# Attention and ReGLU in one kernel: the values of batches 0, 1 and 2 by casting transfers from GpSimd's queue

## The chip, the cores and the metric

The kernel runs on one core of a Trainium2 chip. A core has five engines with instruction queues of their own: TensorE (PE in the profile) for matrix products and for transposes by an identity matrix, VectorE (DVE), ScalarE (ACT), GpSimd (POOL) and SyncE (SP), which here only issues DMA transfers. Each engine takes its instructions in the order of the program, so an instruction that waits holds everything behind it on its engine. The transfers of all queues run on the same 16 DMA engines of the core. The metric is the device time of one execution in microseconds; smaller is better.

## The reference

Eight batches of eight heads, 576 positions, head size 64, all float32. Attention is causal by blocks of 64 positions; its output, turned into 4608 rows of 512, goes through a gated feed-forward layer (FFN).

```
scores = (q @ k^T) / sqrt(64)          # 8 x 8 x 576 x 576
scores = where(block_i >= block_j, scores, -1e9)
attn   = exp(scores - max) / sum
x      = (attn @ v) as 4608 x 512
out    = (relu(x @ w_gate) * (x @ w_val)) @ w_out     # 512 -> 1536 -> 512
```

q, k and v are 9.4 MB each, the three weights 3.1 MB each, and the output 9.4 MB. Matrix products are made in bfloat16, so each input has to be turned from float32 to bfloat16 somewhere between DRAM and TensorE.

## The kernel before, in words

**Tiles.** The 576 positions of a batch are 512 main ones (four chunks of 128) and a tail of 64. A round `r` is one pair of heads of one batch (batch `r // 4`, pair `r % 4`). For a round TensorE makes the scores, transposed, keys on the partitions (`part` for the rounds of batch 0, `visit` after that), ScalarE the exponentials into `attnT`, VectorE or GpSimd sets the masked corners to zero (`corners`), and TensorE multiplies `attnT` with the values (`products_with_v`, L585 main, L599 tail). A 65th column of ones in each head's values gives the sum of the exponentials, by which VectorE divides (`normalise`). The result is transposed into `xT` and is the moving operand of the FFN products: L663 for gate and value, L748 for the output. ScalarE takes the ReLU (L673), VectorE the product `hT` (L679) and the copy of the output (L758).

**Values.** `v_bf` has two buffers, for even and odd batches, 128 partitions x 5 chunks x 8 heads x 65 columns of bfloat16; chunk 4 is the tail. The tail products of batches 0 to 2 are made apart (`tail_visit`, `tail_av` with L547), some time behind the main ones.

**How q, k and v come in.** For batches 3 to 7, `load_qkv` issues casting transfers from GpSimd's queue: the source is float32, the destination bfloat16, one transfer per chunk of 128 positions and 8 heads (L338). For batches 0, 1 and 2 the class `Early` loads float32 into staging buffers from SyncE's queue and casts them on an engine:

- `load_qk` (L140) and `cast_qk` (L195) for q and k. Batches 0 and 1 are then transposed on TensorE (`pe_mains`), batch 2 by SyncE's DMA transposes into `perm` (`transpose`, L242) and copies of these into `qTm` and `kTm` (`unpermute`, L253);
- `load_v` (L159), one transfer per head, and `cast_v` (L220) for the values of batches 0 and 1: per pair of heads in batch 0, per four heads in batch 1;
- `load_v_chunks` (L169) and `cast_v_chunks` (L228), per two chunks, for the values of batch 2;
- `load_tails` and `cast_tails` for the 64 tail positions of all three.

The pool `stage` has ten buffers of 4 KB per partition. Loads of q, k, v and of the weights (L356, cast by L382) and the exponentials of the separate tails (L499) take their turns in it. A transfer into a buffer waits until that buffer's last cast is over. Each queue's completion semaphores are eight in turn, so the ninth transfer of a queue waits for the landing of the first.

**Order.** Nothing is scheduled by the compiler here. The table `AT` gives each action a place, counted in FFN matmuls (negative ones lie before the first), and the actions are issued in the order of these numbers, with FFN matmuls between them as far as the number says. It's an order of issue and not a time: each engine's queue gets its own instructions in this order and runs ahead as far as its waits let it. Names in it that matter here: `Lq..` and `Lv..` load q, k and v of batch 0, `E1..` and `E2..` those of batches 1 and 2, `cq..` and `cv..` cast those of batch 0, `ev..` the values of batch 1, `q2` and `q24` cast and DMA-transpose the first and second half of q and k of batch 2, `u0` to `u3` copy `perm` into `qTm` and `kTm` (`u0` on GpSimd, `u1` and `u2` on VectorE, `u3` on VectorE and ScalarE), `A0` and `B0` are the tail products of batch 0, `v2` casts the values of batch 2, `s8` to `s11` are the scores of batch 2, `l3` and `lv3` load batch 3.

```
for n in sorted(acts, key=lambda n: AT[n]):
    ffn(int(AT[n]) - place[0])
    place[0] = max(place[0], int(AT[n]))
    acts[n]()
```

Of the kernel before, what the change touches and what calls it, by code (L numbers as in the profile page):

```python
# [17 lines left out]
def kernel(  # L18
# [10 lines left out]
    nc = tc.nc  # L29
# [40 lines left out]
    v_bf = [consts.tile([128, NCH, 8, 65], BF, name=f"v_bf{i}") for i in range(2)]  # L70
# [4 lines left out]
    def halves_of(t, par):  # L75

        return t[64 * par : 64 * par + 64].rearrange("p (h g) d -> p g h d", g=2)[
            :, par
        ]
# [29 lines left out]
    def new_bt():  # L109
        return sb.tile([64, 512], BF, name="q_bt", bufs=2)  # L110

    def new_stage(w):
        return sb.tile([128, 1024], FP, name="stage", bufs=10)[:, 0:w]
# [7 lines left out]
    class Early:  # L121
# [32 lines left out]
            self.load(self.st[1, h0], k, h0, n, k_eng)  # L154

        def load_v(self, h0, n):
            st = self.st[2, h0] = new_stage(256 * n)
            for h in range(n):
                nc.sync.dma_start(  # L159
                    st[:, 256 * h : 256 * h + 256].rearrange("p (c d) -> p c d", c=4),  # L160
                    v[self.b, h0 + h, 0:512, :].rearrange("(c p) d -> p c d", p=128),
                )

        def load_v_chunks(self, g):

            st = self.st["c", g] = new_stage(1024)
            for i in range(2):
                s0 = 256 * g + 128 * i
                nc.sync.dma_start(  # L169
                    st[:, 512 * i : 512 * i + 512].rearrange("p (h d) -> p h d", h=8),  # L170
                    v[self.b, :, s0 : s0 + 128, :].rearrange("h p d -> p h d"),
                )

        def load_tails(self, ts):
# [27 lines left out]
        def cast_tails(self, q_too, par, eng):  # L202

            if q_too:
                self.tl = new_bt()
                eng(self.tl, self.st["t", 0])
            eng(
                k_bt[self.b % 2][
                    64 * par : 64 * par + 64, :, 64 * par : 64 * par + 64
                ],  # L210
                self.heads_of(1, par),
            )
            par = 1 - par
            eng(
                halves_of(v_bf[self.b % 2][:, 4, :, :], par)[:, :, 0:64],
                self.heads_of(2, par),
            )

        def cast_v(self, h0, n, eng):
            eng(  # L220
                v_bf[self.b % 2][:, 0:4, h0 : h0 + n, 0:64].rearrange(
                    "p c h d -> p h c d"
                ),
                self.st[2, h0].rearrange("p (h c d) -> p h c d", h=n, c=4),
            )

        def cast_v_chunks(self, g, eng):
            eng(  # L228
                v_bf[self.b % 2][:, 2 * g : 2 * g + 2, :, 0:64],
                self.st["c", g].rearrange("p (c h d) -> p c h d", c=2, h=8),  # L230
            )

        def half(self, t, hg):
# [566 lines left out]
    dve, act, pool = nc.vector.tensor_copy, nc.scalar.copy, nc.gpsimd.tensor_copy  # L800
# [7 lines left out]
    with tc.manual_schedule(engines={E.PE, E.DVE, E.Activation, E.Pool, E.SP}):  # L808

        e0, e1, e2 = [Early(b) for b in range(3)]  # L810
# [45 lines left out]
        zeros_by = {"dve": zero_dve, "pool": zero_pool}  # L856

        def v_2():
            e2.cast_v_chunks(0, pool)
            e2.cast_v_chunks(1, pool)  # L860

        def un(hp):
            return lambda: e2.unpermute(hp, [by[e] for e in HOW[f"u{hp}"]])
# [27 lines left out]
        def mains_1(hp):  # L891
# [8 lines left out]
        AT = {  # L900
            "Lq0": -63.5,
            "Lq2": -62.27,
            "Lv0": -61.59,
            "Lv2": -59.5,
            "Lq6": -59.5,
            "Lq4": -59.5,
            "v00": -58.48,
            "g00": -56.5,
            "Lv4": -54.8,
            "Lv6": -54.8,  # L910
            "g01": -53.5,
            "v10": -53.5,
            "g10": -49.5,
# [14 lines left out]
            "c0": -37.69,  # L928
            "M1k": -37.69,
            "M1q": -37.69,  # L930
            "cv2": -33.09,
            "p11": -32.5,
            "p10": -29.72,
            "M2": -29.71,
            "p12": -29.71,
            "cv0": -29.7,
            "p20": -20.67,
            "p21": -20.67,
            "M3": -20.67,
# [5 lines left out]
            "p22": -20.26,  # L945
            "a1": -17.73,
            "p30": -17.27,
            "cv4": -17.27,
            "b1": -17.03,
            "p32": -13.98,  # L950
            "c2": -13.74,
# [5 lines left out]
            "cg00/23": -4.5,  # L957
            "b2": -4.5,
            "cg01/23": -3.47,
            "cv6": -3.23,  # L960
            "v20": -0.39,
            "g11": -0.39,
            "cv00/01": 4.09,
# [20 lines left out]
            "w11": 32.11,  # L984
            "w20": 32.12,
            "w10": 32.12,
            "E1v0": 32.16,
            "w21": 32.16,
            "E1q6": 32.19,
            "E1q4": 32.19,  # L990
            "E1v4": 32.19,
            "T0": 32.19,
            "E2q0": 32.19,
            "T1": 32.23,
# [6 lines left out]
            "cw21/0": 32.33,  # L1001
            "cw11": 32.33,
            "cw20": 32.33,
            "ev0": 32.33,
            "q6": 32.36,
            "q4": 32.36,
            "E2q4": 33.82,
            "ev4": 34.05,
            "tc0": 34.05,
            "q2": 37.71,  # L1010
            "tc1": 48.64,
# [2 lines left out]
            "m0": 83.51,  # L1014
            "m1": 87.1,
            "s4": 93.79,
            "E2v0": 109.09,
            "cw21/1": 110.84,
            "e4": 114.3,
            "c4": 116.83,  # L1020
# [3 lines left out]
            "e5": 121.28,  # L1024
            "m2": 122.6,
            "c5": 124.67,
            "E2v4": 125.35,
            "T2": 126.26,
            "a5": 127.05,
            "s6": 128.09,  # L1030
# [25 lines left out]
            "L1": 184.04,  # L1056
            "u1": 190.06,
            "u0": 190.06,
            "v2": 191.07,
            "q24": 191.07,  # L1060
            "E1": 194.6,
            "s8": 198.81,
# [121 lines left out]
        acts = {  # L1184
            "Lq0": lambda: e0.load_qk(0, 2, nc.scalar),
            **{f"Lq{h}": lambda h=h: e0.load_qk(h, 2) for h in (2, 4, 6)},
            **{f"Lv{h}": lambda h=h: e0.load_v(h, 2) for h in (0, 2, 4, 6)},
            **{
                n: load(n, load_w_half, i, g, t)
                for i in range(2)  # L1190
# [20 lines left out]
            "j2": lambda: junk(1, 256),  # L1211
            "cq0": lambda: e0.cast_qk(0, 2, (dve, act)),
            **{f"cq{h}": lambda h=h: e0.cast_qk(h, 2, (pool, pool)) for h in (2, 4, 6)},
            **{f"cv{h}": lambda h=h: e0.cast_v(h, 2, pool) for h in (0, 2, 4, 6)},
            "M0": lambda: e0.pe_mains(0, (dve, [(act, 0, 1), (dve, 1, 4)])),
            "M1q": lambda: e0.pe_mains(1, [by[e] for e in HOW["M1"]], ts=(0,)),
            "M1k": lambda: e0.pe_mains(1, [by[e] for e in HOW["M1"]], ts=(1,)),
# [22 lines left out]
            "T2": lambda: load_tails(e2),  # L1240
            "E2q0": lambda: e2.load_qk(0, 4),
            "E2q4": lambda: e2.load_qk(4, 4),
            "E2v0": lambda: e2.load_v_chunks(0),
            "E2v4": lambda: e2.load_v_chunks(1),
            "q0": lambda: e1.cast_qk(0, 4, (pool, None)),
            "k0": lambda: e1.cast_qk(0, 4, (None, by[HOW["k0"]])),
            "q4": lambda: e1.cast_qk(4, 2, [by[e] for e in HOW["q4"]]),
            "q6": lambda: e1.cast_qk(6, 2, [by[e] for e in HOW["q6"]]),
            "ev0": lambda: e1.cast_v(0, 4, pool),
            "ev4": lambda: e1.cast_v(4, 4, pool),  # L1250
            **{f"tc{b}": lambda e=e: e.cast_tails(True, 0, pool) for b, e in enumerate((e0, e1, e2))},
            **{f"td{b}": lambda e=e: e.cast_tails(False, 1, dve) for b, e in enumerate((e0, e1, e2))},
            **{f"m{hp}": lambda hp=hp: mains_1(hp) for hp in range(4)},
# [4 lines left out]
            **{f"o{i}": lambda: late.pop(0)() for i in range(4)},  # L1258
            **{f"u{hp}": un(hp) for hp in range(4)},
            "v2": v_2,  # L1260
            "l3": lambda: load_qkv(3, (0, 1)),
            "t2": e2.transpose_tails,
# [61 lines left out]
```

## Time and profile before

| what | us |
|---|---|
| median of three runs | 362.74 (362.61 to 365.04) |
| span of the profiled execution, first to last instruction | 363.3 |
| TensorE busy | 353.3 |
| TensorE's weight loads busy (beside its products) | 176.9 |
| VectorE busy | 170.7 |
| ScalarE busy | 167.9 |
| GpSimd busy | 112.8 |

The times come from runs without a profile; every duration of one instruction, and every place in time, comes from the one profiled execution. Its span is 0.6 us above the median. In the profile a line of a group or of a timeline names engine, source line, operation, the tile written and the tiles read, the shape and the number of instructions; `[2.42 <-DMA x]` says that the engine sat idle 2.42 us before it and that the transfer of x ended that. A transfer counts as landed when its semaphore says so, later than its issue by the time given under DMA issues: the median is 5.4 us for the float32 loads of v from SyncE's queue, and 6.1 us for the casting loads of v from GpSimd's. The DMA engines' work by queue over the whole span:

```profile
q0 software_dynamic: 70480, 8.85, 46.7%
q1 hardware_dynamic: 76480, 31.86, 44.8%
q10 hardware_dynamic: 5088, 8.78, 7.2%
```

The columns are packets, MB written, and the time that the packets took, as a share of 16 engines' span. q0 is GpSimd's queue, q1 SyncE's and q10 ScalarE's.

### The profile page before, as it was taken

What the parts mean: (1) busy time and instruction counts of PE and PEld (TensorE: products, weight loads), DVE (VectorE), ACT (ScalarE), POOL (GpSimd) and SP (SyncE); (2) the same over time, 40 slices, a digit from 0 to 9 for tenths busy, and PEclk for the clock granted to TensorE, in tenths of its full rate; (3) what the DMA queues carried; (4) which work ended last, traced back from release to release, by engine and by line L of the source; (5) the groups of instructions that cost most, each with busy time, mean ns of one, the idle gap of its engine ahead of it and who ended that gap; (6) DMA issues with size and microseconds to landing.
All of it is one profiled execution on the core that took longest, in us unless ns stands there. A gap on an engine that the chain in (4) does not pass through costs nothing.

```text
span 363.3 us, 7423 instructions
## 1 busy us (share of the span) xinstructions
PE 353.3 (97%) x2933; PEld 176.9 (49%) x2933; DVE 170.7 (47%) x426; ACT 167.9 (46%) x265; POOL 112.8 (31%) x157
## 2 busy tenths in 40 slices
PE   7899999999998999999999999999999999999996
PEld 3544455545544555555555454554455544444443
DVE  4663456677433363444445443554255434333432
ACT  4933676696325850666055625553365403302310
POOL 4647645695209500680049001930000000000000
PEclk9999999999999999999999999999999999999999
DMA  8999999999999995899449951997220130031013
GB/s 245 298 357 374 314 239 255 189 156 138 186 203 108 141 154 137 56 146 186 109 49 145 169 133 46 130 157 152 81 16 14 54 102 0 0 88 29 1 41 105
DMA packets 152083, 49.97 MB, mean 138 GB/s; under 512 B 134512, under 2 KB 145008, under 8 KB 152048
## 3 DMA queue, kind: packets, MB, share of 16 engines
q0 software_dynamic: 70480, 8.85, 46.7%
q1 hardware_dynamic: 76480, 31.86, 44.8%
q10 hardware_dynamic: 5088, 8.78, 7.2%
q8 instruction: 23, 0.38, 0.5%
q14 instruction: 12, 0.10, 0.1%
HBM read 37.75 MB, written 9.44 MB: 130 GB/s over the span
## 4 chain that ended last, share of the span: by engine, by line
PE 89%; DMA 5%; ACT 4%; DVE 1%; issue 0%; POOL 0%; SPq 0%; POOLq 0%; DVEq 0%
PE ffnp L663 49%; PE ffnp L748 23%; PE sc L450 3%; PE ffnp L585 2%; PE one L450 2%; DMA xT<-xnat 2%; DMA stage<-in_moe_w_gate_dram 2%; PE one L585 2%; ACT attnT L414 2%; PE one L663 1%; ACT attnT L455 1%; PE ffnp L547 1%; PE one L794 1%; DMA kTt<-k_bt 1%; PE ffnp L599 1%; PE one L599 1%
## 5 line engine op out<-in xcount | busy, mean ns | idle before, releaser
L679 DVE TENSOR_TENSOR hT<-gate_sb,ffnp 128x512 bf16<-128x512 bf16 x106 | 72.6, 685 | 96.5 <-PE ffnp L663 70.7
L673 ACT ACTIVATE gate_sb<-ffnp 128x512 bf16<-128x512 f32 x103 | 62.1, 605 | 103.3 <-PE ffnp L663 93.6
L663 PE MATMUL ffnp<-xT,wv 128*128 128x512 bf16 x376 | 100.7, 379 | 0.0
L663 PE MATMUL ffnp<-xT,wg 128*128 128x512 bf16 x364 | 99.0, 379 | 1.1 <-DMA xT<-xnat 0.4
L748 PE MATMUL ffnp<-wo,hT 128*128 128x512 bf16 (+2 forms) x444 | 98.8, 373 | 0.0
L748 PEld LDWEIGHTS <-hT 128*128 128x128 bf16 x444 | 41.8, 98 | 45.5 <-issue 0.6
L663 PEld LDWEIGHTS <-wv 128*128 128x128 bf16 x432 | 40.1, 98 | 45.5 <-issue 3.2
L663 PEld LDWEIGHTS <-wg 128*128 128x128 bf16 x432 | 39.8, 98 | 44.6 <-issue 3.6
L455 ACT ACTIVATE attnT<-sc 128x1024 bf16<-128x1024 f32 x56 | 56.8, 1044 | 0.0
L758 DVE COPY ob<-ffnp 128x512 f32<-128x512 f32 (+2 forms) x37 | 25.0, 676 | 45.1 <-PE ffnp L748 44.7
L338 POOL DMA_DIRECT2D q_bf<-in_q_dram x20 | 17.8, 903 | 76.3 <-DVE hT L679 52.0
L462 ACT ACTIVATE attnT<-one 128x512 bf16<-128x512 f32 (+1 forms) x28 | 15.0, 536 | 53.8 <-PE ffnp L450 53.8
L585 PEld LDWEIGHTS <-attnT 128*128 128x128 bf16 x640 | 26.5, 97 | 13.9 <-DVE attnT L803 1.3
L338 POOL DMA_DIRECT2D v_bf<-in_v_dram x30 | 24.3, 853 | 6.8 <-PE one L585 2.2
L450 PEld LDWEIGHTS <-kTm 64*128 64x128 bf16 x384 | 11.3, 94 | 15.6 <-issue 7.8
L338 POOL DMA_DIRECT2D k_bf<-in_k_dram x20 | 17.7, 933 | 0.0
L450 PE MATMUL sc<-qTm,kTm 64*128 64x512 bf16 (+1 forms) x168 | 16.9, 305 | 0.0
L585 PE MATMUL ffnp<-v_bf,attnT 128*128 128x65 bf16 x320 | 15.0, 194 | 0.0
L462 ACT ACTIVATE attnT<-ffnp 128x512 bf16<-128x512 f32 (+1 forms) x28 | 15.0, 534 | 0.0
L803 DVE MEMSET attnT<- 64x128 uint32 x59 | 9.0, 165 | 12.0 <-ACT attnT L455 10.2
L524 DVE TENSOR_TENSOR xnat<-ffnp,recip 128x256 bf16<-128x256 f32 x32 | 13.6, 424 | 1.1
L585 PE MATMUL one<-v_bf,attnT 128*128 128x65 bf16 x250 | 11.6, 193 | 0.7 <-POOL v_bf L220 0.7
(122 smaller groups left out, 293.8 us busy)
## 6 DMA issues: line engine op xcount, KB each, us to landing
out_dram<-ob ACTq DMA_DIRECT2D x29, 256.0 KB, 2.4
stage<-in_moe_w_val_dram SPq DMA_DIRECT2D x6, 512.0 KB, 8.2
stage<-in_moe_w_gate_dram SPq DMA_DIRECT2D x6, 512.0 KB, 8.7
stage<-in_moe_w_out_dram SPq DMA_DIRECT2D x6, 512.0 KB, 10.5
q_bf<-in_q_dram POOLq DMA_DIRECT2D x20, 128.0 KB, 4.3
k_bf<-in_k_dram POOLq DMA_DIRECT2D x20, 128.0 KB, 5.8
v_bf<-in_v_dram POOLq DMA_DIRECT2D x20, 128.0 KB, 6.1
stage<-in_v_dram SPq DMA_DIRECT2D x19, 128.0 KB, 5.4
```

Of the source, the lines that this page charges most:

```text
L338: ins = nc.gpsimd.dma_start(dst, part_of)
L450: nc.tensor.matmul(o, kTm[b % 2][head_of(hh), c, hp, :], qT, start=True, stop=True)
L455: return lambda: nc.scalar.activation(at[:, :, lo : lo + 512], sc, AF.Exp, scale=scale)
L462: nc.scalar.activation(at[:, hh, 1024 : 1024 + w], third[hh][:, 0:w], AF.Exp, scale=scale)
L524: nc.vector.tensor_tensor(out=out, in0=av[:, 0:m, 0:64], in1=recip[:, 0:m].to_broadcast([rows, m, 64]), op=AX.mult,)
L585: nc.tensor.matmul(av[:, p, :], at[:, col : col + 128], v_bf[b % 2][:, c, h, :], start=(p == 0), stop=(c == p), skip_group_check=True,)
L663: nc.tensor.matmul(to, (wg, wv)[t][f // 4][:, c, 128 * (f % 4) : 128 * (f % 4) + 128], x[:, c], start=(c == 0), stop=(c == 3),)
L673: nc.scalar.activation(gate_sb, gate, AF.Relu)
L679: nc.vector.tensor_tensor(out=h, in0=gate_sb, in1=val, op=AX.mult)
L748: nc.tensor.matmul(op, hT[f][:, 128 * s : 128 * (s + 1)], wo[f // 4][:, f % 4, n0:n1], start=(f == 0), stop=(f == 11),)
L758: nc.vector.tensor_copy(ob, op)
L803: nc.vector.memset(o, 0.0)
```

## The change

The main values (chunks 0 to 3) of batches 0, 1 and 2 come by casting transfers from GpSimd's queue, straight into `v_bf`, one per chunk and group of heads: four transfers for all heads of batch 0, four for each half of the heads of batch 1, four for batch 2. The loads from SyncE's queue, their staging buffers and the eight casts on GpSimd are gone. Places in the table change with it: batch 0's values are one action, placed directly before the casts of q and k; batch 1's two actions stand among the casts of the output weights; batch 2's `v2` now issues the transfers, and stands at 184.5 in place of 191.07, so before `u0` and `q24`, where its casts stood behind them.

```diff
         def load_v(self, h0, n):
-            st = self.st[2, h0] = new_stage(256 * n)
-            for h in range(n):
-                nc.sync.dma_start(
-                    st[:, 256 * h : 256 * h + 256].rearrange("p (c d) -> p c d", c=4),
-                    v[self.b, h0 + h, 0:512, :].rearrange("(c p) d -> p c d", p=128),
-                )
-
-        def load_v_chunks(self, g):
...
+            for c in range(4):
+                nc.gpsimd.dma_start(
+                    v_bf[self.b % 2][:, c, h0 : h0 + n, 0:64],
+                    v[self.b, h0 : h0 + n, 128 * c : 128 * c + 128, :].rearrange(
+                        "h p d -> p h d"
+                    ),
                 )
...
-        def cast_v(self, h0, n, eng):
...
-        def cast_v_chunks(self, g, eng):
...
         def v_2():
-            e2.cast_v_chunks(0, pool)
-            e2.cast_v_chunks(1, pool)
+            e2.load_v(0, 8)
...
-            "Lv0": -61.59,
-            "Lv2": -59.5,
+            "Lv0": -47.0,
...
-            "Lv4": -54.8,
-            "Lv6": -54.8,
...
-            "cv2": -33.09,
...
-            "cv0": -29.7,
...
-            "cv4": -17.27,
...
-            "cv6": -3.23,
...
-            "E1v0": 32.16,
+            "E1v0": 32.325,
...
-            "E1v4": 32.19,
+            "E1v4": 32.335,
...
-            "ev0": 32.33,
...
-            "ev4": 34.05,
...
-            "E2v0": 109.09,
...
-            "E2v4": 125.35,
...
-            "v2": 191.07,
+            "v2": 184.5,
...
-            **{f"Lv{h}": lambda h=h: e0.load_v(h, 2) for h in (0, 2, 4, 6)},
+            "Lv0": lambda: e0.load_v(0, 8),
```

More of the change, by code (lines that the diff above doesn't have):

```diff
@@ L156, in load_v @@
         def load_v(self, h0, n):
-            st = self.st[2, h0] = new_stage(256 * n)
-            for h in range(n):
-                nc.sync.dma_start(
-                    st[:, 256 * h : 256 * h + 256].rearrange("p (c d) -> p c d", c=4),
-                    v[self.b, h0 + h, 0:512, :].rearrange("(c p) d -> p c d", p=128),
-                )
-        def load_v_chunks(self, g):
[L166 to L171, printed above, removed]
+            for c in range(4):
[4 more added lines that the diff above has]
+                    ),
                 )
@@ L216, in cast_tails @@
                 self.heads_of(2, par),
-            )
-        def cast_v(self, h0, n, eng):
[L220 to L225, printed above, removed]
-        def cast_v_chunks(self, g, eng):
-            eng(
-                v_bf[self.b % 2][:, 2 * g : 2 * g + 2, :, 0:64],
-                self.st["c", g].rearrange("p (c h d) -> p c h d", c=2, h=8),
             )
@@ L1213 @@
             **{f"cq{h}": lambda h=h: e0.cast_qk(h, 2, (pool, pool)) for h in (2, 4, 6)},
-            **{f"cv{h}": lambda h=h: e0.cast_v(h, 2, pool) for h in (0, 2, 4, 6)},
             "M0": lambda: e0.pe_mains(0, (dve, [(act, 0, 1), (dve, 1, 4)])),
@@ L1242 @@
             "E2q4": lambda: e2.load_qk(4, 4),
-            "E2v0": lambda: e2.load_v_chunks(0),
-            "E2v4": lambda: e2.load_v_chunks(1),
             "q0": lambda: e1.cast_qk(0, 4, (pool, None)),
@@ L1248 @@
             "q6": lambda: e1.cast_qk(6, 2, [by[e] for e in HOW["q6"]]),
-            "ev0": lambda: e1.cast_v(0, 4, pool),
-            "ev4": lambda: e1.cast_v(4, 4, pool),
             **{f"tc{b}": lambda e=e: e.cast_tails(True, 0, pool) for b, e in enumerate((e0, e1, e2))},
```

## The prediction

> **What bounds the kernel now.** First the page's busy times, then its idle groups by stretch: TensorE is the bound, with 353.3 of 363.3 us, at full granted clock in all slices.
>
> ```profile
> PE 353.3 (97%) x2933; PEld 176.9 (49%) x2933; DVE 170.7 (47%) x426; ACT 167.9 (46%) x265; POOL 112.8 (31%) x157
> ```
>
> By stretch TensorE is busy 13.45 of the first 17.43 us (much of it one-off waits between small products), 5.01 of 5.57 up to 23 us, all 37.00 up to 60, 42.63 of 43 up to 103, 15.45 of 17 up to 120 and all 180 after that up to 300. So the order of TensorE's work is fixed and full; any delay put into it before 120 us moves the end one for one, and only a wait that is taken out before 120 us can be won. Two places matter.
>
> **Start.** The chain that ended last, in order of time, goes through a weight transfer here:
>
> ```profile
> 12.98 6.80 DMA stage<-in_moe_w_gate_dram
> 19.80 0.62 ACT wg L382
> 20.42 0.49 ACT xT L629
> 20.96 0.38 PE ffnp L663
> ```
>
> ScalarE ends its exponentials at 16.91, copies xT, and then sits 2.42 us for the gate weights; the reader is to see that ScalarE has slack there, in front of a DMA. The instructions in order of time on ScalarE and GpSimd show the work before it:
>
> ```profile
> 10.49 0.61 POOL L195 CAST k_bf<-stage 128x512 bf16<-128x512 f32 x1
> 11.59 1.18 POOL L220 CAST v_bf<-stage 128x512 bf16<-128x512 f32 x2 [0.49 <-DMA stage<-in_v_dram]
> ```
> ```profile
> 11.53 0.61 ACT L278 COPY qTm<-ffnp 128x512 bf16<-128x512 bf16 x1
> 12.00 4.91 ACT L414 ACTIVATE attnT<-sc 128x1024 bf16<-128x1024 f32 x6
> 19.80 0.62 ACT L382 CAST wg<-stage 128x512 bf16<-128x512 f32 x1 [2.42 <-DMA stage<-in_moe_w_gate_dram]
> ```
>
> The last q and k pair (heads 6, 7) is cast 10.49 to 11.10, TensorE transposes it at once, ScalarE copies it at 11.53 and starts its last six exponentials at 12.00: nothing is idle in this chain. The DMA engines are at 9 tenths in every slice of 3 to 20 us.
>
> **Middle.** GpSimd in order of time, then VectorE and TensorE:
>
> ```profile
> 66.06 1.08 POOL L253 COPY qTm<-perm 128x512 bf16<-128x512 bf16 x1 [4.75 <-DMA perm<-q_bf]
> 67.11 1.08 POOL L253 COPY kTm<-perm 128x512 bf16<-128x512 bf16 x1
> 68.13 1.04 POOL L195 CAST q_bf<-stage 128x1024 bf16<-128x1024 f32 x1
> 69.12 1.04 POOL L195 CAST k_bf<-stage 128x1024 bf16<-128x1024 f32 x1
> 70.10 1.04 POOL L228 CAST v_bf<-stage 128x1024 bf16<-128x1024 f32 x1
> 71.92 1.04 POOL L228 CAST v_bf<-stage 128x1024 bf16<-128x1024 f32 x1 [0.77 <-PE one L472]
> ...
> 75.42 3.67 POOL L338 DMA_DIRECT2D q_bf<-in_q_dram  x4
> ```
> ```profile
> 78.51 0.90 DVE L253 COPY kTm<-perm 128x512 bf16<-128x512 bf16 x1
> 79.33 0.68 DVE L679 TENSOR_TENSOR hT<-gate_sb,ffnp 128x512 bf16<-128x512 bf16 x1
> ```
> ```profile
> 69.40 0.28 PE L547 MATMUL ffnp<-v_bf,stage 128*128 128x65 bf16 x4
> 74.76 0.28 PE L450 MATMUL one<-qTm,kTm 64*128 64x256 bf16 x1
> 80.06 1.02 PE L663 MATMUL ffnp<-xT,wv 128*128 128x512 bf16 x4
> ```
>
> GpSimd runs ahead: it copies batch 2's first head pair (66.06) 8.7 us before its scores (74.76), casts the second half of q and k by 70.16, and only behind that writes batch 2's values into the buffer that batch 0's tail products (L547) read until 69.5. The casts release SyncE's transposes (issued 71.88 and 74.10, landing 4.2 and 3.6 us later, 76.11 and 77.74), which VectorE copies at 77.99 and 78.51, 0.8 us behind the landing; the hT product behind them ends at 80.01 and frees the PSUM buffer of the matmul at 80.06. There is no slack from 78.5 to 80.06.
>
> **The change part by part.**
>
> *Removed:* eight casts on GpSimd, four of 0.6 to 0.8, two of 1.05, two of 1.04 us, 6.8 us in all; 20 SyncE issues; eight staging buffers. GpSimd is busy 31%, so the casts alone are worth nothing on the path. The staging buffers let weights queue sooner: the gate half that landed at 19.78 was issued at 12.98 and can now go at about 6 to 7. Its gain is bounded: from 18.12 TensorE has, without any wait, 3 matmuls (0.65), 20 products (0.62), 4 transposes (0.22), 4 matmuls (0.87) ahead of the one at 20.96, which ends at 20.48. At most 0.5 us.
>
> *Added at the start:* four casting issues of batch 0 at the head of GpSimd's queue, behind the memset that VectorE ends at 2.16. The same form in the trace (128x8x64) takes 0.89 to 1.03 us, 3.6 for four: 2.25 to 5.9, so the cast at 5.35 starts at 5.9. Its first packets follow 2.4 us behind the issue (75.42, 77.9), so from 4.65 all of v passes: 4 x 0.9 = 3.6 us of DMA time (from 111 to 118 us this queue alone moves 6462 packets, some 1000 per us). Before, only two of the eight v loads were ahead of the last k, 2 x 0.57 (131 KB at 230 GB/s) = 1.1 us. So the last k lands 2.5 us later, 12.8 instead of 10.3, and the exponentials end at 19.3 instead of 16.9. From there: VectorE's corner memset 0.17 and xT 0.42 (20.0), then the 2.36 us of TensorE listed above: 22.4 instead of 20.96. **+1.5 us**; ScalarE's 2.42 us wait swallows the rest. Bounds: -0.5 (q and k lose nothing) and +6 (the two queues alternate packet by packet: 4096 packets of v pass beside 4096 of 1 KB, which alone move at 350 per us, 11.7 + 3.6 us, v landing near 20.8, where the first product now starts at 12.82). I stay near the row: from 80 to 85 us the casting queue moved 3671 packets beside 288 of stores, so it isn't the one that starves.
>
> The Trainium skill (DMA: Bandwidth & Descriptors, Queues, rings and completion order) says that each DMA engine goes round its queues and drains a whole packet, typically 9 to 17 descriptors, before it switches; if a casting packet held 9 to 17 rows at 14 ns against one 51 ns packet of q and k, v would take 70 to 80% of the time (an estimate from that page and these two rows), and the sum would stay as it is.
>
> *Added at 40 to 52 us (batch 1):* eight issues of 512 rows between the weight casts. The nearest row, 512 rows into 64 partitions, takes 0.72; 8 x 0.72 = 5.7 us against 2.1 of casts removed. Four stand ahead of three wo casts: these end at 46.6 instead of 45.0, needed at 45.6 to 46.1 before, 47.1 to 47.6 with the start's +1.5. The casts of heads 4, 5 end at 50.6; TensorE's transposes of them were at 49.07, now 50.57. **+0.1** (0 to 1.6, if an issue takes 0.9).
>
> *Moved in the middle (batch 2):* four issues now stand ahead of the two copies at 66.06 and the two casts at 68.13, and have to wait for the buffer's last reader, the product that ends at 69.55. Queued behind them on GpSimd: copies, casts, tails, batch 3's loads. In the old clock: 69.6 + 3.67 (four issues, row 75.42) = 73.3; copies 2.1, 75.4 (scores at 74.76: 0.65 late); casts 2.0, ending 76.4 and 77.4; SyncE 76.4 instead of 71.88, second landing 5.86 later (71.88 to 77.74) at 82.3; VectorE's copy 0.6 and hT 0.68, 83.6 instead of 80.01. TensorE waits at 80.06 until 83.6. **+3.5 us**, the 0.65 included. Low end 2.4 (SyncE issues the second transpose after 1.28 instead of 2.1 us), high end 4.5 (transposes took 8.0 and 6.1 beside other transfers at 57.9). Batch 3's sixteen loads start 3.7 us later, as TensorE does; what TensorE waits at 102 to 120 (1.9 us, for transposes that run beside them) stays, 0 (-1 to +1).
>
> [...]
>
> **Sum:** 1.5 + 0.1 + 3.5 = +5.1 us on a span of 363.3, 368.4. The span lies 0.6 above the median of the runs, 362.74; there it is **367.8**. One per cent (3.6 us) is about what this kernel's runs can tell from no change.
>
> **Rivals.**
> 1. *Only the middle costs* (A: start between -0.5 and +0.5). For: ScalarE's wait. Against: the chain 10.49 to 16.91 has no gap. 362.74 + 3.5 = 366.2. Chance 0.17.
> 2. *Only the start costs*: the second half's transposes land in time. For: VectorE's load there falls. Against: 0.8 us of slack for 4.5. 364.3. Chance 0.10.
> 3. *Not slower:* the wait at batch 2 isn't felt, because the four issues pass GpSimd quickly or its transposes come quicker; decided at VectorE's copy at 78.51: it must not be over 0.8 us later than now. Then the start's bounded gain of 0.5 is left: 362.2; with the 1.9 us at 102 to 120 gone as well, 360.4. Chance 0.10.
> 4. *v starves at the start* behind q, k and weights: first product at 20 us, +6 + 3.5: 372. Chance 0.08.
> That the transfers don't cast or don't move is excluded by the order of the built program: the casts are gone, the issues stand where I said.
>
> **Chances.** Forecast (366.4 to 370) 0.55. Range: rivals 3 and 4 stay outside (0.18); the lower end takes in rival 2's start without 1 us of a wait at 102 to 120, 363.3; the upper end +1.6 (batch 1), +1 (middle) and +1 at 102 to 120, 371.6. Faster by over 1%: 0.04 (out of rival 3). Slower by over 1%: the forecast, rival 4 and part of rival 1, 0.68. Within 1%: 0.28.
>
> **What would show it.** Right: ScalarE's last six exponentials start near 14.4 and its wait for gate weights is gone; on GpSimd the batch 2 issues start at TensorE's last L547 product of batch 0 and the two qTm/kTm copies follow; VectorE waits for perm at the second kTm copy some 3 to 4 us and TensorE idles before the matmul that was at 80.06. Wrong: q and k cast as early as now; or the copies not behind the issues; or an issue far from 0.9 us.

## The result

The changed kernel takes 379.85 us (median of five runs, 379.25 to 380.12), the kernel before 362.97 us in the same comparison (five runs, 362.61 to 365.04). The ratio is 1.044, with a 95% interval of 1.041 to 1.047: 16.9 us slower. The forecast was 367.8 us, with a range up to 371.6. The sign was right and the size was not.

The profiled execution of the changed kernel has a span of 377.4 us and belongs to a run of 379.25. TensorE's busy time and its granted clock, from the page of the changed kernel:

```profile
PE 355.5 (94%) x2933; PEld 178.4 (47%) x2933; DVE 170.4 (45%) x426; ACT 168.3 (45%) x265; POOL 119.5 (32%) x165
...
PEclk9858999999999999999999999999999999999999
```

TensorE does the same work and still bounds the kernel, but it is busy 94% of the span and not 97%, and in the second to fourth slices (of 9.4 us each), above all the third, it doesn't get its full clock. Its longest waits by releaser (us in total, times, longest):

```profile
PE one L562 <- DMA v_bf<-in_v_dram: 10.7, 3, 4.1
...
PE one L449 <- DMA kTt<-k_bt: 1.1, 1, 1.1
```

The first line is the loss at the start, and it names a transfer that the forecast did not have on the path: the values themselves. TensorE, GpSimd and ScalarE there, in order of time:

```profile
12.56 0.24 PE L562 MATMUL one<-v_bf,attnT 128*128 128x65 bf16 x2
15.60 0.25 PE L562 MATMUL one<-v_bf,attnT 128*128 128x65 bf16 x3 [2.81 <-DMA v_bf<-in_v_dram]
19.91 0.38 PE L562 MATMUL one<-v_bf,attnT 128*128 128x65 bf16 x4 [4.05 <-DMA v_bf<-in_v_dram]
24.12 0.21 PE L562 MATMUL one<-v_bf,attnT 128*128 128x65 bf16 x1 [3.84 <-DMA v_bf<-in_v_dram]
24.15 0.73 PE L562 MATMUL ffnp<-v_bf,attnT 128*128 128x65 bf16 x10
```
```profile
2.47 3.67 POOL L158 DMA_DIRECT2D v_bf<-in_v_dram  x4 [1.15 <-DVE v_bf L90]
...
11.02 0.61 POOL L186 CAST k_bf<-stage 128x512 bf16<-128x512 f32 x1
```
```profile
12.45 1.94 ACT L391 ACTIVATE attnT<-sc 128x1024 bf16<-128x1024 f32 x2
25.25 3.22 ACT L391 ACTIVATE attnT<-sc 128x512 bf16<-128x512 f32 x4 [10.87 <-PE sc L377]
```

The last k of batch 0 lands 0.2 us later (10.56, 10.32 before) and is cast at 11.02 (10.49 before), so q and k lose half a microsecond; ScalarE starts its last exponentials at 12.45 (12.00 before). But the first product of one head needs all four chunks, and it gets them at 12.56, 15.60, 19.91 and 24.12. ScalarE's old wait for gate weights is now a wait of 10.87 us for the scores that stand behind this product on TensorE.

Followed instruction by instruction, TensorE is at most 0.6 late up to 12.8 us (time of the first profile of before), 11.0 late at 13.09, 12.05 late at 21.61, and stays so up to batch 2. There, GpSimd, VectorE and TensorE:

```profile
81.93 3.58 POOL L158 DMA_DIRECT2D v_bf<-in_v_dram  x4 [19.90 <-PE ffnp L524]
85.55 1.18 POOL L230 COPY qTm<-perm 128x512 bf16<-128x512 bf16 x1
86.68 1.04 POOL L230 COPY kTm<-perm 128x512 bf16<-128x512 bf16 x1
```
```profile
92.02 0.62 DVE L230 COPY qTm<-perm 128x512 bf16<-128x512 bf16 x1 [1.04 <-DMA perm<-q_bf]
93.27 0.59 DVE L230 COPY kTm<-perm 128x512 bf16<-128x512 bf16 x1 [0.64 <-DMA perm<-k_bf]
```
```profile
87.78 0.28 PE L427 MATMUL one<-qTm,kTm 64*128 64x256 bf16 x1 [0.92 <-POOL kTm L230]
94.52 1.02 PE L640 MATMUL ffnp<-xT,wv 128*128 128x512 bf16 x4 [1.54 <-DVE hT L656]
```

The matmul that was at 74.76 is 13.0 late, the one that was at 80.06 is 14.5 late: 2.4 us more. At 109.0 TensorE has 0.7 us back, and at the end it is 13.9 late.

That is 14.1 us between the spans, and 16.9 between the medians. The difference lies in the base. In the runs whose time and span are both known, 1.7 to 1.95 us lie around the span (379.25 and 377.4, for one), so the first profile of before, 363.3, fits a run of some 365.1 us, as the one of 365.04 was, and not one near the median. A second profile of the same kernel, taken for this comparison, has 360.7 and belongs to a run of 362.52:

> The kernel before once more, for a second profiled execution. The first one, whose span of 363.3 us was the base of the prediction, has 1.9 us of waits between 102 and 120 us which most of the experiments' profiles don't have. Theory (these waits belong to that execution and not to the kernel): without them the span is 361 to 361.8 us, some 1.8 us below a time of 362.6 to 363. Rival (they are always there): a span of 362.8 us or more, with waits of TensorE for transposes between 102 and 120 us.

The span lies just below the range of the theory, and 2 us below the rival's. The rows give the stretch, its length, the busy time and instructions of TensorE, its weight loads, VectorE, ScalarE and GpSimd, and last the granted clock, the DMA share and GB/s. First the old profile, then the new one of the same kernel:

```profile
98.00:112.00 14.00, 12.19 (x116) 5.71 (x109) 4.05 (x7) 6.11 (x9) 2.31 (x3) 1.00 1.14 178
```
```profile
98.00:112.00 14.00, 13.89 (x131) 6.97 (x125) 4.74 (x8) 7.48 (x13) 3.12 (x4) 1.00 1.01 157
```

The two agree within 0.3 us to 102 us; then the old one loses 2.6 us up to 111.8, with waits for transposes, and nothing after that. The new one has no wait for a transpose there. So executions of the kernel before differ by these waits. The new profile is that of one of the shortest runs, 0.45 us below the median of the comparison (362.97), so a median run has few of them or none; which isn't shown. Against the new profile the change costs 12.05 us at the start, 1.0 and 1.5 at batch 2, and 2.0 between 102 and 110 us (1.1 of it the wait for kTt above): 16.5, within 0.4 us of the difference of the medians. Why the changed kernel waits between 102 and 110 us isn't shown.

### The profile page after: what moved, and what is told of

Read it like the earlier page. It is cut to its first block, busy times and chain, and to the rows that moved or that the text cites. A ratio compares the mean times of both kernels' runs of the same rounds, so it can differ in the third digit from the quotient of the medians.

```text
span 377.4 us, 7397 instructions
## 1 busy us (share of the span) xinstructions
PE 355.5 (94%) x2933; PEld 178.4 (47%) x2933; DVE 170.4 (45%) x426; ACT 168.3 (45%) x265; POOL 119.5 (32%) x165
## 3 DMA queue, kind: packets, MB, share of 16 engines
q0 software_dynamic: 83024, 10.43, 52.5%
## 4 chain that ended last, share of the span: by engine, by line
PE 82%; DMA 10%; DVE 2%; ACT 2%; POOL 1%; SPq 1%; issue 1%; DVEq 0%; POOLq 0%
PE ffnp L640 46%; PE ffnp L725 22%; DMA stage<-in_moe_w_gate_dram 5%; PE sc L427 3%; DMA xT<-xnat 2%; PE ffnp L562 2%; PE one L427 2%; PE one L562 2%; SPq L333 1%; PE one L640 1%; DMA stage<-in_k_dram 1%; ACT attnT L432 1%; DMA kTt<-k_bt 1%; PE ffnp L576 1%; DMA perm<-k_bf 1%; PE ffnp L524 1%
## 5 line engine op out<-in xcount | busy, mean ns | idle before, releaser
L432 ACT ACTIVATE attnT<-sc 128x1024 bf16<-128x1024 f32 x56 | 56.7, 1041 | 0.0
L562 PEld LDWEIGHTS <-attnT 128*128 128x128 bf16 x640 | 28.0, 100 | 24.5 <-issue 12.3
L315 POOL DMA_DIRECT2D v_bf<-in_v_dram x30 | 24.3, 858 | 4.2 <-DMA k_bt<-in_k_dram 2.0
L562 PE MATMUL one<-v_bf,attnT 128*128 128x65 bf16 x250 | 12.8, 198 | 10.7 <-DMA v_bf<-in_v_dram 10.7
L158 POOL DMA_DIRECT2D v_bf<-in_v_dram x16 | 13.3, 848 | 21.1 <-PE ffnp L524 19.9
L315 POOL DMA_DIRECT2D k_bf<-in_k_dram x20 | 17.7, 928 | 0.0
L562 PE MATMUL ffnp<-v_bf,attnT 128*128 128x65 bf16 x320 | 15.8, 199 | 0.0
L391 ACT ACTIVATE attnT<-sc 128x1024 bf16<-128x1024 f32 (+1 forms) x12 | 10.1, 880 | 11.8 <-PE sc L377 11.4
```

The lines of the kernel that those rows point to most:

```text
L158: nc.gpsimd.dma_start(v_bf[self.b % 2][:, c, h0 : h0 + n, 0:64], v[self.b, h0 : h0 + n, 128 * c : 128 * c + 128, :].rearrange("h p d -> p h d"
L315: ins = nc.gpsimd.dma_start(dst, part_of)
L391: nc.scalar.activation(attnT[r % 4][:, :, 512 * i : 512 * i + w], sc[:, :, 0:w], AF.Exp, scale=scale)
L432: return lambda: nc.scalar.activation(at[:, :, lo : lo + 512], sc, AF.Exp, scale=scale)
L562: nc.tensor.matmul(av[:, p, :], at[:, col : col + 128], v_bf[b % 2][:, c, h, :], start=(p == 0), stop=(c == p), skip_group_check=True,)
```

## The experiments

Each time stands against runs of the kernel before on the same chip; its medians were 363.22, 362.89 and 363.83 in the three comparisons.

**Batch 0 alone.** Four casting transfers for batch 0 as in the change (`load_v_cast` is what the change calls `load_v`); batches 1 and 2 as before.

```diff
-            **{f"Lv{h}": lambda h=h: e0.load_v(h, 2) for h in (0, 2, 4, 6)},
+            "Lv0": lambda: e0.load_v_cast(0, 8),
-            **{f"cv{h}": lambda h=h: e0.cast_v(h, 2, pool) for h in (0, 2, 4, 6)},
```

> Only batch 0's values come by casting transfers; batches 1 and 2 are as before. Theory: the whole start is due to this part alone, v's four transfers landing some 4.2 us apart, the last near 24 us, and TensorE's FFN matmul that was at 20.96 some 11.6 us late. The middle has no added wait, so some 0.7 us of the waits at 102 to 120 us come back at most: 374 to 375.5 us, against 379.85 for the whole change and 362.97 before. Rival (the places share the loss, for instance because fewer staging buffers are taken by batches 1 and 2 and weights come earlier and in the way of v): v lands earlier than 22 us and the time is under 372 us.

Measured: 374.9 us, ratio 1.031 (1.027 to 1.035), 11.7 us slower. The last v landed at 24.5, and TensorE was 12 to 13 us behind the second profile of before from there to the end. The start is its own loss. How the two queues share the DMA engines is read from the packets of the changed kernel between 12 and 20 us (queue, packets, MB written, share of 16 engines):

```profile
q1 hardware_dynamic: 1952, 1.94, 88.1%
q0 software_dynamic: 1951, 0.25, 46.7%
```

As many packets of the one as of the other. SyncE's carry 1 KB, GpSimd's one row of 64 values, 256 bytes read and 128 written. So v gets 245 rows per us, as long as SyncE has weights queued.

**Is it the sharing, or is a casting transfer slow?** In the next kernel SyncE's first weight transfer waits until v has landed, so that v has only q and k beside it (`held` is the last of the four v transfers). The four also stand earlier in the table, but GpSimd issues them at the same time as with batch 0 alone (2.46 us).

```diff
-        nc.sync.dma_start(st, view.rearrange("(c p) f -> p c f", p=128))
+        ins = nc.sync.dma_start(st, view.rearrange("(c p) f -> p c f", p=128))
+        if held:
+            after(ins, held.pop())
```

> As the kernel with batch 0's values alone by casting transfers, but the first transfer of FFN weights on SyncE's queue waits until the last of the four value transfers has landed, and the four are issued some instructions earlier. SyncE's queue then has only q and k beside v. Theory (the two queues take turns, one packet for one packet, so that v lands late because SyncE's queue is long and not because casting transfers are slow): q and k pass in the same turns, v has the engines to itself once they are through, and the last v lands at 13 to 16 us in place of 24; the weights come some 5 us later than before, and the time is 363.5 to 369 us. Rival (a casting queue of 256-byte rows moves no more than some 245 packets per us at this place, because GpSimd writes its descriptors slowly or starts cold): v's last landing stays at 22 to 24 us, the weights come behind it, and the time is 380 us or more.

Measured: 367.06 us, ratio 1.009 (1.005 to 1.013). Its profile is that of its longest execution (371.94), so only the landings are read from it, not the waits further on. Packets from 10 to 13 us, and the time from issue to landing of the four transfers (least, median, longest):

```profile
q0 software_dynamic: 2394, 0.30, 157.7%
q1 hardware_dynamic: 1, 0.00, 0.0%
```
```profile
DMA to landing us min/median/max: 8.1/8.3/8.4
```

With the other queue empty v moves 800 packets per us over these 3 us, 1224 in the first of them, and the last one lands at 13.6. In the changed kernel the same row reads

```profile
DMA to landing us min/median/max: 8.9/13.8/18.9
```

so a casting transfer isn't slow; it waits its turn. In this execution TensorE then waited 2.86 us for gate weights at 17.7 instead, which is where its loss begins.

**Does one packet go for one packet, whatever its size?** All weight transfers with rows of 1 KB are cut in two, with rows of 512 bytes.

```diff
+        n = 128 if st.shape[2] == 256 else 512
+        for lo in range(0, st.shape[2], n):
+            nc.sync.dma_start(st[:, :, lo : lo + n], src[:, :, lo : lo + n])
```

> As the kernel with batch 0's values alone by casting transfers, but every weight transfer whose rows are 1 KB long goes as two transfers of 512-byte rows, so that SyncE's packets are half as long and twice as many. Theory (one packet for one packet): a pair of packets takes less time, 31 ns for v's and about 35 to 40 instead of 59 for SyncE's, so v moves 330 to 400 packets per us beside the weights instead of 245; the last v lands at 18 to 21 us in place of 24, and the time is 3 to 6 us below that of the kernel with batch 0 alone, in as far as the weights are not what TensorE then waits for. Rival (the queues share by bytes or by time, or v has a rate of its own): the last v lands at 24 us or later, and the time is the same or longer.

Measured: 371.46 us, ratio 1.022 (1.019 to 1.025), 3.4 us below batch 0 alone. Packets from 10 to 14 us:

```profile
q1 hardware_dynamic: 1338, 0.68, 82.9%
q0 software_dynamic: 1361, 0.17, 65.3%
```
Still one for one, at 340 per us each instead of 245 (the changed kernel's row above); SyncE's bytes fall from 0.24 to 0.17 MB per us. The last v lands at 20.9, and at 24.5 with batch 0 alone. A share by bytes, or by time, would not have let v through faster.

**The same queue without casting.** Batch 0's eight float32 loads are issued from GpSimd's queue, into the same buffers, with the same casts behind them.

```diff
+            queue = nc.gpsimd if self.b == 0 else nc.sync
             for h in range(n):
-                nc.sync.dma_start(
+                queue.dma_start(
```

> The kernel before with one thing changed: the eight float32 loads of batch 0's values are issued from GpSimd's queue and not from SyncE's. They don't cast; they go into the same staging buffers and are cast on GpSimd as before. Theory (the loss at the start is that of a second queue whose 256-byte rows take turns with SyncE's 1-KB packets): the last v lands at 21 to 25 us, as by casting transfers, and the time is 371 to 377 us. Rival (it is casting that makes the transfers late): v lands by 16 us and the time is 363 to 366 us.

Measured: 368.46 us, ratio 1.014 (1.009 to 1.019), and the last v landed at 14.55. On v the rival was right, though not on the time: a second queue alone doesn't make v late. The packets from 8 to 12 us:

```profile
q0 software_dynamic: 213, 0.61, 56.6%
q1 hardware_dynamic: 491, 0.48, 52.3%
```
Without a cast GpSimd's packets are large (2.9 KB in the mean, most of them 4 KB, that is 16 rows of 256 bytes), so one packet can move 16 rows. The two queues don't go one for one here (213 to 491); by what rule they share isn't shown. Now q and k are late: eight issues take GpSimd 6.1 us ahead of their casts, the last k landed at 13.5 (10.3 before) and was cast 3.1 us later, 2.0 of it by the issues and 1.1 by the landing, and TensorE was 2.9 us late at 12.82. Late q and k are the picture the forecast had for the start, with another kind of transfer. The profile, that of the shortest run (365.84), shows little loss beyond this (3.4 us at the end, against the second profile of before); the median is 2.6 us higher, and where that lies isn't shown.

**Batches 1 and 2 alone**, with batch 0 as before (the edits of the change for these two).

> Only batches 1 and 2 change; batch 0 is loaded and cast as before. Theory: TensorE is as before up to 74 us, then the four issues ahead of the two copies of batch 2 cost what they cost in the whole change, +2.4 us, with some 0.7 us given back at 102 to 120 us: 364.5 to 365.5 us. The prediction's own sum for these two parts, +3.6, would give 366.5 us. Rival (the middle costs only because the start is late, since the casts and the transposes meet other work then): no difference from before, 363 us.

Measured: 372.88 us, ratio 1.025 (1.022 to 1.029). This is 9.7 us, four times what I expected, and with the 11.7 of batch 0 it is more than the whole change costs. Against the second profile of before TensorE is 4.45 us late from 50 to 74 us, loses 2.4 at batch 2 as in the whole change, and 3.5 more between 102 and 112 us, with waits of 0.65 and 2.23 us for transposes of batch 3's k, whose cause isn't shown. So the parts don't add, and the loss before 74 us, nothing in the changed kernel, is large here. Its TensorE between 46 and 53 us, and a row of its granted clock (third number from the end):

```profile
46.41 4.64 PE L758 MATMUL ffnp<-wo,hT 128*128 128x512 bf16 x13 [2.13 <-POOL wo L392]
...
52.40 0.53 PE L595 MATMUL one<-v_bf,attnT 128*128 128x65 bf16 x5 [0.22 <-DMA v_bf<-in_v_dram]
```
```profile
48.00:50.00 2.00, 2.00 (x6) 0.72 (x5) 0.00 (x0) 0.00 (x0) 2.00 (x4) 0.54 2.60 132
```

It waits for a cast of wo behind the first four issues of batch 1, and then runs at half its clock from 46.4 to 49.8 us (0.61 and 0.54 are means of 2 us that take in some full clock).

**Batch 1 alone.**

```diff
-            "E1v0": lambda: e1.load_v(0, 4),
-            "E1v4": lambda: e1.load_v(4, 4),
+            "E1v0": lambda: e1.load_v_cast(0, 4),
+            "E1v4": lambda: e1.load_v_cast(4, 4),
-            "ev0": lambda: e1.cast_v(0, 4, pool),
-            "ev4": lambda: e1.cast_v(4, 4, pool),
```

> Only batch 1's values come by casting transfers. With batches 1 and 2 changed and batch 0 as before, TensorE waited 2.13 us for a cast of wo behind the first four issues on GpSimd, ran at half clock for some 4 us after that wait, and waited 0.22 us for v: 4.3 us in all. Theory (this cost is batch 1's own and is hidden in the whole change only because the start is some 12 us late): 4.3 us again, 366.5 to 368.5 us. Rival (the prediction's sum for this part, +0.1, is right and the wait came from batch 2's missing float32 loads, which let other transfers go sooner): 362.5 to 364 us.

Measured: 367.16 us, ratio 1.012 (1.009 to 1.015), 4.3 us, as the theory had it.

```profile
46.46 2.96 PE L758 MATMUL ffnp<-wo,hT 128*128 128x512 bf16 x13 [2.03 <-POOL wo L392]
...
50.80 0.22 PE L595 MATMUL one<-v_bf,attnT 128*128 128x65 bf16 x2 [0.40 <-DMA v_bf<-in_v_dram]
...
52.24 0.53 PE L595 MATMUL one<-v_bf,attnT 128*128 128x65 bf16 x5 [0.75 <-DMA v_bf<-in_v_dram]
```

Here the clock doesn't fall after the wait, the thirteen matmuls take 2.96 us and not 4.64, and TensorE waits for v instead: it goes on at 52.24, where the kernel above goes on at 52.40. Issued from 42.24 on, the first four transfers land 7.9 to 8.4 us later, the last at 52.5; the products stood at 47.97. The landing ends the stretch, and the wait for wo lies inside it.

**Batch 1 with its first four issues behind the casts of wo.**

```diff
-            "E1v0": 32.325,
+            "E1v0": 32.331,
```

> Only batch 1 by casting transfers, with its first four issues behind the last three casts of wo on GpSimd and not ahead of them. Theory (the landing of the values is what ends last in batch 1, and the wait for wo lies inside it): TensorE doesn't wait for wo at 44 us any more, the values are issued 2.6 us later and land near 55 us, TensorE waits for them, and the time is 2 to 4 us longer than with the issues ahead: 369 to 371.5 us. Rival (what the prediction looked at, the casts of wo behind the issues, sets batch 1's cost): 363 to 364.5 us.

Measured: 373.27 us, ratio 1.023 (1.017 to 1.028), longer than either expected. The wait for wo is gone, and the values, issued 2.6 us later, cost far more:

```profile
52.83 0.62 PE L595 MATMUL one<-v_bf,attnT 128*128 128x65 bf16 x7 [1.53 <-DMA v_bf<-in_v_dram]
56.76 0.21 PE L595 MATMUL one<-v_bf,attnT 128*128 128x65 bf16 x1 [3.32 <-DMA v_bf<-in_v_dram]
```

The first chunk landed at 50.94, where TensorE had waited 1.97 us, the last at 56.72; the clock was 0.69 in the mean from 51 to 57 us and 0.50 to 60. Earlier casts of wo didn't help and later values cost more: the landing decides. The size beyond the expectation is the later landing (56.7 and not 55) and the clock.

**Batch 1 with all eight issues earlier**, ahead of casts of the FFN weights.

```diff
-            "E1v0": 32.325,
-            "E1v4": 32.335,
+            "E1v0": 32.16,
+            "E1v4": 32.17,
```

> Only batch 1 by casting transfers, with all eight issues where its float32 loads were issued before, some 10 us earlier on GpSimd, ahead of casts of the FFN weights. Theory (taking turns with SyncE's 1-KB packets of wo): the values land before they are needed at 48 us, but the 3072 packets of wo then pass at 245 instead of 350 per us, 12.5 us for 8.8, so wo lands up to 3.8 us later, and TensorE, which had its wo casts just in time, waits for them: 365.5 to 368 us. Rival (only the lateness of the issues costs): 362.5 to 364 us, as before.

Measured: 370.02 us, ratio 1.015 (1.010 to 1.021): outside both, and for a reason in neither. The four chunks that TensorE needed first landed by 48.7 us and kept nothing waiting, since TensorE was late by then (before, it needed them at 47.97), and wo was only 1.4 us late, but the eight issues kept GpSimd itself from its casts for 6.2 us, and TensorE was 7 us late from there on. GpSimd and TensorE:

```profile
32.48 6.20 POOL L176 DMA_DIRECT2D v_bf<-in_v_dram  x8
38.62 1.65 POOL L392 CAST wv<-stage 128x1024 bf16<-128x1024 f32 x2
```
```profile
39.77 1.89 PE L673 MATMUL ffnp<-xT,wv 128*128 128x512 bf16 x4 [5.38 <-POOL wv L392]
```

All three places that were tried for batch 1 cost 4 us or more.

**Batches 0 and 1 together**, batch 2 as before.

> Batches 0 and 1 by casting transfers, batch 2 as before. Alone, batch 0 costs 11.7 us and batch 1 4.3 us. Theory (batch 1's values land at the same time whether the start is late or not, so its 4.3 us lie inside the start's 11.7): 374 to 376 us, the time of batch 0 alone, and no wait of TensorE for v or wo between 40 and 70 us. Rival (the costs add, and it is batch 2's that is hidden in the whole change): 378 to 380 us.

Measured: 375.7 us, ratio 1.031 (1.026 to 1.037). Batch 0 alone has 1.031, so batch 1 adds nothing, and TensorE has no wait of 0.2 us or more between 40 and 75 us. The 12 us at the start hide its 4.3.

**Batch 2 alone**, its issues ahead of the copies as in the change, and **batch 2 alone with the issues behind them**, where the casts were (without the last two lines of the diff).

```diff
         def v_2():
-            e2.cast_v_chunks(0, pool)
-            e2.cast_v_chunks(1, pool)
+            e2.load_v_cast(0, 8)
...
-            "v2": 191.07,
+            "v2": 184.5,
```

> Only batch 2's values come by casting transfers, with their four issues ahead of the two copies and two casts on GpSimd, as in the change. Theory: TensorE is late by 0.9 us at batch 2's scores and by some 1.5 more at the FFN matmul behind the hT product, +2.4 us: 365 to 366.5 us. The prediction's sum for this part, +3.5, would give 366.7 us with the 4.5 of its upper bound 367.7 us. Rival (the cost in the middle comes out of what batches 0 or 1 delay): 363 us.

> As the kernel with batch 2 alone by casting transfers, but the four issues stand behind the two copies and two casts on GpSimd, where the casts of the values stood before. Theory (the place of the issues is the whole cost of batch 2): 362.5 to 363.7 us, no difference from before. Rival (casting transfers beside the DMA transposes or the next batch's loads cost of themselves, wherever they are issued): 364.5 us or more.

Measured: 367.56 us ahead (ratio 1.013, 1.010 to 1.015), 1 us above the upper end of the theory, and 365.22 behind (1.007, 1.004 to 1.010), as the rival had it. So the place isn't the whole cost: behind the copies it still costs 2.3 us. VectorE's second copy and the time from issue to landing of the two transposes, first with the issues ahead, then behind:

```profile
81.39 0.59 DVE L263 COPY kTm<-perm 128x512 bf16<-128x512 bf16 x1 [0.62 <-DMA perm<-k_bf]
```
```profile
perm<-q_bf SPq DMA_TRANSPOSE x1, 3.2
perm<-k_bf SPq DMA_TRANSPOSE x1, 3.1
```
```profile
81.18 0.59 DVE L263 COPY kTm<-perm 128x512 bf16<-128x512 bf16 x1 [1.34 <-DMA perm<-k_bf]
```
```profile
perm<-q_bf SPq DMA_TRANSPOSE x1, 7.3
perm<-k_bf SPq DMA_TRANSPOSE x1, 7.9
```

Ahead, GpSimd casts q and k late, but the transposes then run with little beside them (3.2 and 3.1 us against 4.2 and 3.6 before). Behind, they are issued as early as before and run at the time of the casting transfers of v and of batch 3's loads, and take twice as long. The second copy starts at 81.39 or 81.18, and at 78.51 before. The kernel with the issues ahead loses another 2.2 us between 102 and 110 us, that with the issues behind nothing there. In the first, batch 3's loads start 3.75 us later (79.17 instead of 75.42), in the second not; that this is the cause was not tested.

No version with casting transfers in place of these loads was as fast as the kernel before.

## Why the prediction was wrong

**The start, +1.5 forecast, 12.05 measured: the failed step.** The issues went as the sum had it (2.47 to 6.1 us, 3.67 in all). What failed is the choice between its two bounds. The sum let v pass quickly and q and k wait, by the row at 80 to 85 us, where 3671 casting packets stood beside 288 of stores. In that row the other queue had few packets to send, so it shows what one queue does alone. The upper bound, two queues that alternate packet by packet, is what took place. The text named the sign that would speak against its choice, q and k cast as early as now, and they were 0.5 us late.

That bound, and rival 4 with it, was undersized too: +6. The last v landed at 24.08 and not 20.8: v's first packet passed at 6.4 us and not at 4.65 (3.9 us behind its issue; the place it took 2.4 from has 1.9, 75.42 to 77.33), a pair of packets passes at 245 per us, where the sum of the two queues' separate rates gives 267, and from 21 us on v's packets thin out to 144, 69 and 22 per us, the last at 23.7 (why isn't shown). Its own terms, 15.3 us from 4.65 on, end near 20 and not at 20.8, and it doesn't say why the 7 to 8 us from 12.82 to there are only 6. The product that stood at 13 needs the last chunk, so the loss is counted from 13 to 24.1 and not less. On top, TensorE's clock was at half until 30 us:

```profile
17.43:23.00 5.57, 0.38 (x4) 0.27 (x4) 0.00 (x0) 0.00 (x0) 0.00 (x0) 0.50 1.29 296
23.00:30.00 7.00, 5.88 (x70) 4.24 (x70) 3.93 (x14) 4.14 (x6) 1.91 (x3) 0.50 0.76 265
```

Between 24.1 and 29.3 TensorE falls 1.4 us further behind without a wait to speak of; a group of ten small products takes 0.73 us there and 0.46 at full clock.

The Trainium skill (DMA: Bandwidth & Descriptors, Queues, rings and completion order), from which the prediction estimated 70 to 80% of the time for v, says that an engine goes round its queues by whole packets of typically 9 to 17 descriptors. Turns by packets are what the rows with casting transfers show. But a casting packet here held one row, so v had a good third of the time (46.7 beside 88.1 in the row of 12 to 20 us), and only the loads without a cast had up to 16.

**Batch 1, +0.1 forecast, 0 measured: right number, wrong reason.** The step priced the issues and the casts behind them, and left out when the values land, 8 us behind their issue. Its casts of wo are too early as well: four issues at its 0.72 us take 2.9 us and not the 1.6 from 45.0 to 46.6, and with batch 1 alone they ended at 47.94. Alone batch 1 costs 4.3 us. It is 0 by luck, because TensorE comes 12 us late (batches 0 and 1 together show it). Had the start cost 1.5 as forecast, some 2.8 of it would have been felt (an estimate, 4.3 less 1.5, not run).

**The middle, +3.5 forecast, 2.4 measured: mechanism right, one term too large.** The issues began behind TensorE's last product of batch 0's tails, the copies followed, the scores were 1.0 us late (0.65 forecast), VectorE waited for both transposes. The term that was too large is the 5.86 us from the first transpose's issue to the second's landing, taken from before; it measured 4.5 (88.73 to 93.25). SyncE issued the second 1.34 us behind the first and not 2.22, which the text had as its low end (its terms make that 2.7 us, not 2.4), and the second landed 3.18 us behind its issue and not 3.64. Rival 1 had this mechanism alone.

**The waits at 102 to 120 us, "stay", 0 (-1 to +1).** Against the first profile TensorE got 0.7 us back there, inside that bound. But the base had 2.6 us of waits that the second profile of before hasn't, and the changed kernel loses 2.0 there. The forecast took the span's 0.6 us above the median as the distance of that run; with what lies around a span it is 2.4.

**The sum of the miss.** Forecast and result differ by 12.05 us: 10.55 at the start, -0.1 at batch 1, -1.1 in the middle, -0.7 at 102 to 120 us, 0.35 after that and at the ends of the span, and 3.0 from the base (2.4 from before's run, 0.6 since the profile after is that of a run 0.6 below its median). That the miss and the loss at the start are both 12.05 is chance. The chances were misplaced most at rival 4: the case that took place had 0.08. The range's upper end, 371.6, adds up to 371.4 from the terms it names; the result lies far above either.

## What to carry to other kernels

Before a transfer is moved to another queue, look at what the old and the new queue hold at that moment: with both backed up and the moved transfers casting short rows, count turns and not bytes, and price the moved transfer by its small packets beside the other queue's large ones. A row taken where the other queue was nearly idle tells nothing of that. Price the landing of moved data against its first use, not only the issue, and price each part as if the others were not there, since a loss early on hides those behind it; and compare the profiled run's own time with the median before its waits are taken as the kernel's.

## What was not expected of the hardware

- Two backed-up queues, one of them with casting transfers, shared the DMA engines one packet for one packet, at 1 KB and at 512 bytes beside 128 (1952 to 1951 and 1338 to 1361). With plain packets of up to 4 KB it was 213 to 491. A casting transfer sent one row of 256 bytes per packet, a plain one from the same queue up to 4 KB.
- TensorE's clock fell to half around waits: 0.50 after waits of 2.8 to 4.1 us at the start, 0.50 for 3.4 us after one of 2.13 us at 44 us, but 1.00 after one of 2.03 us at the same place in another kernel. Where the values arrived last anyway, this cost next to nothing (52.40 against 52.24). The Trainium skill (TensorE: Matmul & The Clock Gate, Part 1: The HAM clock gate) puts the fall behind an idle window of about 3.4 us; the wait of 2.13 us was shorter and was enough.
